# Chunked attention and a Swish feed-forward on one core: AV joined with the next scores, two halves turned by DMA, and the DMA queues planned anew

## The chip, the cores and the metric

The kernel runs on one core of a Trainium2 chip. The metric is the time on the device in microseconds (us), as the median of several executions. The kernel before took 303.95 us (302.63 to 308.57, four runs). Wherever two kernels are compared as a ratio, it is the mean time of one kernel's fast runs over the mean of the other's fast runs of the same rounds, so it is not quite the ratio of the medians that stand beside it. Differences of under 2% count as "same"; where less is claimed, the 95% interval is given.

Engines in the lines of the profile: PE is TensorE's matmul, PEld its weight load, DVE is VectorE, ACT ScalarE, POOL GpSimd, SP SyncE (here it only issues DMAs). A "q" after the name is the engine's sequencer.

## The reference, cut to what matters

```python
# q, k, v: (8 batches, 8 heads, 576 tokens, 64), float32; attention inside chunks of 64 tokens
scores = q_c @ k_c.T / 8 ; attn = softmax(scores) ; x = attn @ v_c      # x: 4608 tokens x 512
h = x @ w_in                                                            # 512 -> 2048
out = (h * sigmoid(beta * h)) @ w_out                                   # 2048 -> 512
```

The two dense products are nearly all the work. The kernel cuts the 4608 tokens into 9 blocks of 512, and each block into two halves of 256 tokens (halves 0 to 17). A block's first product (called mm1) needs both of its halves through attention; its second product (mm2) is interleaved with mm1 of the next block.

## The kernel before

The instructions' order on each engine is not written by hand. While the kernel is built, every piece of work is put into a list with its dependencies and an estimated time, and a small simulation on the host (called "the planner" here) plays the list through. The order in which its simulated engines start the pieces becomes the fixed order of the real ones. The chip then follows this order whatever happens: each engine waits for the semaphores of its next instruction and does nothing else meanwhile.

```python
def schedule(self):                       # the planner, at build time
    ...
    if kind == "dma":                     # us = (issue time on the queue, packets, ns of one packet)
        free[e] = t + us[0]
        u["packets"], u["ns"], u["arrive"] = us[1], us[2], t + 2.0
    ...
    # one DMA server for both queues, at most 64 packets at a time:
    server = t + m * u["ns"] * 1.07e-3
    ... finished(u, server + 0.9)
    # engines: among what is ready at the time, PE, SP and POOL take the lowest rank
    u = min(ready, key=lambda u: (u["rank"] ..., u["seq"]))
# [...]
P.dma(queue, (0.62, 64, 21.5), ...)       # v: half of a half's v
P.dma("sp", (2.5, 128, 27), ...)          # q and k of a half turned by a DMA transpose
P.dma("sp", (1.23, 64, 21), ...)          # x of a half turned by a DMA transpose
```

A half goes this way. SP loads q, k, v (256 KB DMAs). POOL casts q and k to bf16. Halves 0 to 5 are transposed on PE, halves 6 to 17 by a DMA transpose on SP's queue, after which POOL reorders them (two copies into `qkO`). Then PE computes the scores, ACT the exponentials, PE the product with v (AV), DVE divides by the row sum, and x is turned once more (PE or DMA) into `xT`, which mm1 reads.

```python
def attention(h, turn, ...):              # h < 6: turn == "pe", else "dma"
    ...                                   # casts, transposes, reorders
    go(r, scores, h, (0, 1), slack=0.5)   # 32 matmuls of 64x64 on four quadrants of the array
    go(0, exp, h, (0, 1))
    go(r, attend, h, (0, 1), slack=0.4)   # AV: 32 matmuls of 64x64
    for u in range(2):
        go(0, normalize, h, u)
    go(-2, turn_x_dma, h)
```

PSUM's eight banks: A0, A1 for scores, A2, A3 (and A0, A1 again) for AV, F0, F1 for mm1, F2, F3 for mm2.

The softmax here doesn't subtract the row's maximum and nothing guards it: scores larger than these inputs give would overflow.

## Time and profile before

| | before |
|---|---|
| median, us | 303.95 |
| span of the profiled run, us | 300.3 |
| PE busy | 93% |
| granted TensorE clock | 1.00 |

These are lines of the page of the kernel before: the span, the busy times (us, share of the span, instructions), then the span in 40 equal slices with PE's busy share and the granted TensorE clock in tenths, and the share of each engine in the chain of work that ended last.

```profile
span 300.3 us, 6155 instructions
...
PE 279.9 (93%) x2544; PEld 143.9 (48%) x2578; DVE 144.8 (48%) x264; ACT 153.6 (51%) x242; POOL 113.6 (38%) x117
...
PE   0799997999999999999999999999999999999995
...
PEclk9999999999999999999999999999999999999999
...
PE 86%; DMA 5%; DVE 4%; issue 2%; POOLq 1%; ACT 1%; SPq 0%; POOL 0%; DVEq 0%
```

PE is busy from the second slice to the last. The longest waits of PE in the kernel before (who waited for whom, us in total, times, longest):

```profile
PE F L482 <- DVE qkb L332: 7.7, 1, 7.7
PE A L527 <- ACT E L536: 1.4, 2, 0.7
...
PE A L527 <- POOL qkO L332: 0.8, 1, 0.8
```

The first wait is the start of the kernel. After it PE hardly ever waits for attention's data; its one wait for POOL's reorder is 0.8 us. This is how one half stands in PE's stream (start, duration, engine, line, what, how many): L605 is mm1, L634 mm2, L527 scores, L552 AV.

```profile
128.64 0.81 PE L605 MATMUL F<-xT,w_in_bf 128*128 128x512 bf16 x3
129.38 0.44 PE L527 MATMUL A<-qkO 64*64 64x64 bf16 x32
129.76 1.04 PE L605 MATMUL F<-xT,w_in_bf 128*128 128x512 bf16 x4
...
132.46 0.45 PE L552 MATMUL A<-v_bf,E 64*64 64x65 bf16 x32
```

A dense matmul of 512 columns starts every 0.216 us, and attention's two visits of about 0.5 us each lie between them without an idle gap.

### The profile page before, as it was taken

To read this page: it belongs to the slowest core of one execution; us is meant where nothing else is said; L and a number is where in the kernel's file an instruction comes from. 1 tells how busy PE (TensorE), PEld (TensorE's weight loads), DVE (VectorE), ACT (ScalarE), POOL (GpSimd) and SP (SyncE) were. 2 spreads that over 40 slices of the span, in tenths; PEclk is the share of its full clock that TensorE was granted. 3 is DMA by queue.
4 is the path that set the end of the run, shared out by engine and by line. 5 is a ranking of instruction groups with operands and counts; after the bars stand their busy time and mean duration, and the time that the engine had idled before them with its cause. 6 is when DMAs were issued, how large, how long until landed. Compare 5 with 4: busy or idle time off the path is not lost.

```text
span 300.3 us, 6155 instructions
## 1 busy us (share of the span) xinstructions
PE 279.9 (93%) x2544; PEld 143.9 (48%) x2578; DVE 144.8 (48%) x264; ACT 153.6 (51%) x242; POOL 113.6 (38%) x117
## 2 busy tenths in 40 slices
PE   0799997999999999999999999999999999999995
PEld 0575444666654444444444444444444444444444
DVE  0467905685547633464555645355353453443300
ACT  2548614875656724564664555554455545545311
POOL 1534344436576570665636375512512410000000
PEclk9999999999999999999999999999999999999999
DMA  6999399899998998999999999457636622111133
GB/s 225 283 386 403 113 294 289 255 274 263 264 264 221 214 218 186 248 191 219 222 198 251 177 256 181 103 129 160 155 108 148 132 52 55 37 35 35 46 87 79
DMA packets 94795, 55.98 MB, mean 186 GB/s; under 512 B 77736, under 2 KB 78000, under 8 KB 94768
## 3 DMA queue, kind: packets, MB, share of 16 engines
q1 hardware_dynamic: 94016, 54.41, 74.9%
q10 hardware_dynamic: 752, 1.19, 1.3%
q8 instruction: 20, 0.33, 0.4%
q14 instruction: 7, 0.06, 0.1%
HBM read 36.71 MB, written 9.44 MB: 154 GB/s over the span
## 4 chain that ended last, share of the span: by engine, by line
PE 86%; DMA 5%; DVE 4%; issue 2%; POOLq 1%; ACT 1%; SPq 0%; POOL 0%; DVEq 0%
PE F L634 38%; PE F L605 30%; PE F L609 5%; PE A L605 3%; PE A L527 3%; PE A L552 2%; DMA qkstage<-in_q_dram 2%; DMA qkT<-qkb 2%; DVE qkO L332 1%; DVE xn L566 1%; PE A L482 1%; PE A L574 1%; DMA wstage<-in_v_dram 1%; PE F L482 1%; POOLq L830 1%
## 5 line engine op out<-in xcount | busy, mean ns | idle before, releaser
L634 PE MATMUL F<-w_out_bf,g 128*128 128x512 bf16 (+1 forms) x558 | 136.0, 373 | 2.6 <-issue 1.1
L625 DVE SCALAR_TENSOR_TENSOR g<-tt,F 128x512 bf16<-128x512 bf16 (+1 forms) x148 | 91.7, 628 | 96.4 <-ACT tt L622 96.2
L622 ACT ACTIVATE tt<-F,beta_half 128x512 bf16<-128x512 f32 (+1 forms) x148 | 93.6, 641 | 86.9 <-PE F L605 78.7
L605 PE MATMUL F<-xT,w_in_bf 128*128 128x512 bf16 x448 | 111.2, 379 | 0.0
L634 PEld LDWEIGHTS F<-w_out_bf,g 128*128 128x128 bf16 x592 | 56.5, 98 | 61.2 <-DVE w_out_bf L332 0.2
L605 PEld LDWEIGHTS F<-xT,w_in_bf 128*128 128x128 bf16 x448 | 42.1, 98 | 50.8 <-DVE g L625 5.6
L332 POOL COPY qkO<-qkT 128x1024 bf16<-128x1024 bf16 x24 | 46.5, 1967 | 29.5 <-DMA qkT<-qkb 29.5
L332 POOL CAST qkb<-qkstage 128x1024 bf16<-128x1024 f32 x30 | 30.7, 1041 | 37.3 <-DMA qkstage<-in_q_dram 26.9
L330 ACT ACTIVATE ostage<-F 128x512 f32<-128x512 f32 (+1 forms) x36 | 21.3, 591 | 24.3 <-PE F L634 24.3
L332 POOL CAST v_bf<-vstage 128x512 bf16<-128x512 f32 x32 | 19.5, 613 | 20.1 <-DMA vstage<-in_v_dram 19.9
L566 DVE TENSOR_TENSOR xn<-A,R 128x512 bf16<-128x512 f32 x36 | 24.9, 691 | 1.2
L536 ACT ACTIVATE E<-A 128x512 bf16<-128x512 f32 (+1 forms) x24 | 19.4, 808 | 8.8 <-PE A L527 8.8
L609 PE MATMUL F<-xT,w_in_bf 128*128 128x256 bf16 x160 | 20.5, 273 | 0.0
L609 PEld LDWEIGHTS F<-xT,w_in_bf 128*128 128x128 bf16 x160 | 14.9, 98 | 3.5 <-DVE g L625 0.9
L564 DVE RECIPROCAL R<-A 128x8 f32<-128x8 f32 x36 | 7.3, 202 | 16.8 <-PE A L552 16.3
L527 PE MATMUL A<-qkO 64*64 64x64 bf16 x576 | 9.4, 199 | 4.4 <-ACT E L536 1.4
L332 POOL CAST qkb<-wstage 128x1024 bf16<-128x1024 f32 x4 | 4.2, 1040 | 22.6 <-DMA wstage<-in_k_dram 13.6
L527 PEld LDWEIGHTS A<-qkO 64*64 64x64 bf16 x576 | 6.7, 110 | 12.4 <-issue 4.7
L482 PE MATMUL F<-ident,qkb 128*128 128x128 bf16 x32 | 3.8, 312 | 7.7 <-DVE qkb L332 7.7
L605 PE MATMUL A<-xT,w_in_bf 128*128 128x512 bf16 x48 | 10.7, 379 | 0.0
L332 DVE COPY qkO<-A 128x1024 bf16<-128x1024 bf16 x4 | 4.9, 1224 | 10.5 <-PE A L482 10.5
L552 PEld LDWEIGHTS A<-v_bf,E 64*64 64x64 bf16 x576 | 6.6, 109 | 6.6 <-ACT tt L622 3.0
(43 smaller groups left out, 98.5 us busy)
## 6 DMA issues: line engine op xcount, KB each, us to landing
out_dram<-ostage SPq DMA_DIRECT2D x70, 128.0 KB, 2.4
qkstage<-in_q_dram SPq DMA_DIRECT2D x32, 256.0 KB, 4.4
vstage<-in_v_dram SPq DMA_DIRECT2D x32, 256.0 KB, 5.1
qkstage<-in_k_dram SPq DMA_DIRECT2D x28, 256.0 KB, 4.5
wstage<-in_moe_w_in_dram SPq DMA_DIRECT2D x4, 1024.0 KB, 13.2
g<-in_moe_w_out_dram SPq DMA_DIRECT2D x2, 1024.0 KB, 12.4
qkstage<-in_k_dram ACTq DMA_DIRECT2D x4, 256.0 KB
vstage<-in_moe_w_out_dram SPq DMA_DIRECT2D x1, 1024.0 KB, 15.0
```

Source lines behind the costliest of these rows:

```text
L330: P.op("act", us, lambda e: e.activation(dst, src, AF.Copy, **kw), reads, writes)
L332: P.op(eng, us, lambda e: e.tensor_copy(dst, src), reads, writes)
L482: P.op("pe", 0.056, lambda e, i=i: e.transpose(dst[:, i, :], qkb[:, s, which, i, :], ident[:, :]), reads=[K("qkb", s, which, i // 4, v=h), ...
L527: return e.matmul(bank(hb)[64 * c2:64 * c2 + 64, 64 * i:64 * i + 64], qkO[r, s, 1, hp, 64 * c:64 * c + 64], qkO[r, s, 0, hp, 64 * c:64 * c ...
L536: P.op("act", act_us(128 * (b - a)), lambda e: e.activation(E[:, s, :, a:b, :].rearrange("p g i q -> p g (i q)"), A[:, 0:2, 64 * a:64 * b] ...
L552: return e.matmul(bank((A2, A0)[u] + c2)[64 * hb:64 * hb + 64, j:j + 65], E[r, s, hb, i, :], v_bf[r, sv, 2 * hv + cp, 4 * hb + hp, 0:65])
L566: P.op("dve", 0.7, lambda e: e.tensor_tensor(xn[:, s, u, :, :, :].rearrange("p c k (h d) -> p c (k h) d", h=2), o[:, :, :, 0:64], R[:, 2 * ...
L605: return e.matmul(bank(n).rearrange("p (v c t) -> p v c t", v=2, c=4), w, xT[:, sx, :, u, :, 64 * hb:64 * hb + 64], start=(kt == 0), stop= ...
L609: return e.matmul(bank(n)[:, 256 * hv:256 * hv + 256].rearrange("p (c t) -> p c t", c=4), w, xT[:, sx, hv, u, :, 64 * hb:64 * hb + 64], st ...
L622: P.op("act", 0.075 + act_us(N), lambda e: e.activation(tt[:, T % 3, c], bank(n)[:, c], AF.Tanh, scale=beta_half[:, t:t + 1]), reads=[K("p ...
L625: P.op("dve", dve_us(N), lambda e: e.scalar_tensor_tensor(g2[:, sg, t, c], tt[:, T % 3, c], 1.0, bank(n)[:, c], ALU.add, ALU.mult), reads= ...
L634: P.op("pe", 0.2158 * (b - a) / 512, lambda e, t=t: e.matmul(bank(n)[:, 0:b - a], g2[:, sg, t, 128 * s:128 * s + 128], w_out_bf[:, t, a:b] ...
```

## The change

Its intent was to save PE time and to start loads better:

1. AV of half h (from 8 on) is joined with the scores of half h + 1 to one visit, so that PE changes its tiling half as often. The last two of the sixteen pairs of results find no room in A2 and A3 and take bank F3; mm2 keeps F2 alone from block 2 on. Both row halves of the array write that bank, so the second of them is put after the scores with a wait on PE's own semaphore.
2. Halves 4 and 5 are turned by DMA and POOL instead of by PE.
3. The start: v of half 0 is loaded before q and k of half 1, over two queues, and halves 0 and 1 are cast and turned in another order. A layout in which v holds token pairs is in the code but switched off ("v kept in one-token rows").
4. Loads of halves 6 to 15 wait for a gate (the Swish step) of an earlier block instead of standing in line.
5. The planner's estimates of DMA time are replaced.

The diff also holds three smaller things: the planner's cost of PE's visits is raised (by 0.2 us for a scores visit of a steady half, 0.4 for its AV, 0.2 for a joined visit), DMA transposes go first among SP's ready pieces instead of standing in line with the loads (`go(-3, turn_dma, h)` in the cut), and mm1 waits for both parts of a half's x.

```diff
-                u["packets"], u["ns"], u["arrive"] = us[1], us[2], t + 2.0
+                u["packets"], u["ns"] = us[1], us[2]
+                u["arrive"] = t + (2.0 if t < 5 else max(1.2, us[0] - 1.0))
 # estimates (issue us, packets, ns of a packet):
-  load_v     (0.62, 64, 21.5)      +  load_v     (0.62, 64, 15.3)
-  load_w_in  (0.62, 32, 91)        +  load_w_in  (0.62, 32, 86)
-  load_w_out (0.62, 16, 176)       +  load_w_out (0.62, 16, 149)
-  turn_dma   (2.5, 128, 27)        +  turn_dma   (2.5, 128, 14.6)
-  turn_x_dma (1.23, 64, 21)        +  turn_x_dma (1.23, 64, 16)
-  put        (0.6, 4, 92)          +  put        (0.6, 4, 78)
 # [... PSUM banks renamed, layouts of xn and xT, pair path (off) ...]
+        def attend_and_score(h):
+            first = attend_main(h)            # 30 of 32 AV matmuls
+            scores(h + 1, (0, 1), A0, 0)
+            attend_rest(h, first)             # the last 2, after `first` has ended
+        FIRST = 8 ; TURNED = 4 ; PAIRS = False
+        def steady(h):
+            ...
+            go(-3, turn_dma, h)               # before: in line with the loads
+            if h < FIRST + 1:
+                go(r, scores, h, (0, 1), slack=0.4)
+            else:
+                go(r, attend_and_score, h - 1, slack=0.4)
+                go(0, normalize_all, h - 1)
+                go(-2, turn_x_dma, h - 1)
 # [...]
-                        load_half(h)
+                        load_half(h, after=gated[divmod(16 * (blk - 1) + (TA, TB)[h % 2], 16)])
-                m = F3 if blk == 2 else F2 + s % 2
+                m = (F3 if blk == 2 else FS[2 + s % 2]) if 2 * blk + 2 < FIRST else F2
```

## The prediction

> **What bounds the kernel.** TensorE (PE): the page gives it 93% of a 300.3 us span, no other engine over 51%; the chain of waits is 86% PE. In the chain a run of four 128x512 matmuls takes 0.86 us, 0.216 each; the two dense products need 1152, 249 us. The other 51 us, from the start times in the engine timeline: 20.5 us before the first dense matmul (L609), 3.5 us after the last start, the rest attention between dense matmuls, with its stalls.
>
> A steady half holds PE twice (scores x32, AV x32) for 0.5 us. Only 0.27 us of that is matmuls (8.3 ns each); 0.09 us is lost before, 0.035 inside, 0.12 after. The Trainium skill, "TensorEngine Tiling (Array Packing)", Key Properties, says that a change of tiling mode drains TensorE; the trace agrees: 0.25 us per visit. Halves 4 (60.7 to 68 us) and 5 (78 to 87 us), turned on PE, each add 24 transposes (1.3 us) and about 1.7 us of lost starts, waiting in the timeline for DVE qkO (0.45) and DVE xn (0.5): 3.5 us against 1.0 for a steady half.
>
> **What changes.**
> 1. Joining AV of halves 8 to 16 with scores of 9 to 17: nine visits fewer, 9 x 0.245 = -2.2 us. The unit that waits for PE's own semaphore comes some 60 matmuls later: no bubble.
> 2. Halves 4, 5 by DMA: 2 x (3.5 - 1.0) = -5 us of PE work. But block 2 waits for a longer chain: half 5's loads land at 69.4 us; two Pool casts (1.04), DMA transpose (5.5), two Pool reorders (1.97), scores, exp, AV, division and x's transpose (4.1) end near 89 us; block 2's dense work began at 87.6 before. PE, with 7 us of block 1's mm2 as filler, would get there near 88: a stall of 0 to 3 us, +1.5.
> 3. Start: v of half 0 before q, k of half 1, over two queues: dense work 0.5 to 1.5 us earlier, and the weights with it: -1.
> 4. The join takes a PSUM bank: mm2 of blocks 2 to 7 has F2 alone, so each of 24 swaps waits for ACT's eviction (0.59 us, behind a tanh of 0.64), which one mm1 group (0.86 us) mostly hides: 0.05 us each, +1.2.
> 5. Queues: DMA is near 1.0 busy from 40 to 190 us, but steady blocks are barely starved (one loss of 0.99 us at 239.5): 0.
>
> "One-token rows" changes nothing: the pair path is switched off.
>
> **Sum.** -5.5 us: 298.4 us, 80% range 295 to 302. Faster by over 2% 0.36, within 2% 0.61, slower 0.03.
>
> **What would show it.** (1) Joined visits of 0.8 us instead of 2 x 0.5, nine fewer. (2) 32 q/k and 16 x transposes fewer on PE; whether block 2's first mm1 waits for a DMA of xT. (3) The first 128x256 matmul near 19.5 us. (4) PE waiting for ACT ostage at the first matmul of an mm2 group. (5) PE waiting for Pool qkO near 240 us: the last halves had 5 us of slack, which a faster PE eats.
>
> **What would make it wrong.** If halves 4, 5 are loaded earlier, step 2 brings all 5 us (below 297). If transposes slow the loads in the busiest DMA stage, block 2 stalls by over 3 us. If a swap stalls 0.2 us, the gain of joining is gone.

## The result, and the profile after

The changed kernel took 329.88 us (329.18 to 332.46, four runs), ratio 1.0884 with a 95% interval of 1.0803 to 1.0966: 26 us slower, far outside the predicted range of 295 to 302. The same lines of its page:

```profile
span 327.6 us, 6075 instructions
...
PE 287.6 (88%) x2499; PEld 145.1 (44%) x2530; DVE 144.0 (44%) x264; ACT 151.3 (46%) x234; POOL 119.6 (37%) x119
...
PE   1579989989759989996999799868999999999996
...
PEclk9999999999976999998799999996999999999999
...
PE 48%; DMA 24%; POOL 11%; SPq 7%; issue 4%; DVE 2%; ACT 2%; ACTq 1%; POOLq 0%
```

PE's row has holes all along, and the chain that ended last, 86% PE before, is now only 48% PE: it runs through DMA, POOL and the queue. The granted clock is cut in three places of the row. PE's waits after:

```profile
PE A L587 <- POOL qkO L334: 15.8, 8, 4.2
PE F L492 <- DVE qkb L334: 8.4, 3, 6.7
PE F L702 <- DMA xT<-xn: 3.9, 1, 3.9
```

L587 is the scores, L702 mm1. Eight times PE arrives at a half's scores and POOL has not yet written that half's `qkO`. One such visit in the engine timeline of the changed kernel (L610 is AV, L731 mm2), and the entry to block 2:

```profile
90.38 0.59 PE L587 MATMUL A<-qkO 64*64 64x64 bf16 x32 [2.29 <-POOL qkO L334]
90.91 2.65 PE L731 MATMUL A<-w_out_bf,g 128*128 128x512 bf16 x6
...
94.35 0.47 PE L610 MATMUL A<-v_bf,E 64*64 64x65 bf16 x32
98.68 5.28 PE L702 MATMUL F<-xT,w_in_bf 128*128 128x512 bf16 x12 [3.86 <-DMA xT<-xn]
...
149.99 0.44 PE L610 MATMUL A<-v_bf,E 64*64 64x65 bf16 x30
153.68 0.64 PE L587 MATMUL A<-qkO 64*64 64x64 bf16 x32 [3.25 <-POOL qkO L334]
154.13 0.24 PE L610 MATMUL A<-v_bf,E 64*64 64x65 bf16 x2
154.30 1.89 PE L702 MATMUL F<-xT,w_in_bf 128*128 128x512 bf16 x4
```

The bracket holds the idle time before an instruction and what ended it. At 150 us the 30 AV matmuls run, PE stands for 3.25 us, and only then come the scores and the last two AV matmuls. After it four mm1 matmuls take 1.89 us instead of 1.03: the clock is halved. The Trainium skill, "TensorE: Matmul & The Clock Gate", "What's actually happening", says that an idle window of some 3.4 us takes the array to half rate until it has been busy for as long. The trace agrees on the half rate and on how it ends: after this stall dense matmuls start 0.427 us apart instead of 0.216 until 159.3 us, for about 5 us. It does not need a whole idle window, though: the clock was cut at 152.47 us, when PE had been idle for 2.0 us (more on this in the last section).

Summed over the start times in the trace (after the start-up, gaps over 0.55 us before a PE instruction beyond its normal spacing): 22.9 us of stalls and 7.6 us at half clock in the changed kernel, against 5.2 and 0 in the kernel before. That is 25.3 of the 27.3 us between the two spans. So the loss is PE waiting for attention's data, and the clock that follows from it. The question is why the data come late.

Since the order comes from the planner, its simulated times can be set beside the trace. This table holds, for odd halves, the end of POOL's second reorder, after which the scores can start (us; read from the planner as the kernel is built, and from the trace; the two last kernels are experiments below):

```
half                              7      9     11     13     15
before            planned     101.7  126.5  150.5  176.1  192.0
                  on the chip  98.0  124.1  149.6  176.0  192.1
changed           planned      89.8  111.9  133.5  160.5  192.2
                  on the chip 100.0  126.7  153.6  184.7  222.5
before_fast       planned      86.1  104.1  121.4  137.9  151.9
                  on the chip  94.6  117.8  139.9  162.1  180.8
const             planned     106.5  128.6  150.1  180.5  210.4
                  on the chip 103.6  123.5  146.8  180.3  212.4
```

In the kernel before the chip is up to 4 us ahead of the plan, so PE finds its data ready. In the changed one it is 10 us behind at half 7 and 30 us behind at half 15. The planner had promised 295.9 us for the changed kernel and 295.2 us for the one before.

### The profile page after: what moved, and what is told of

It reads as the page before. It is cut to its first block, busy times and chain, and to the rows that moved or that the text cites. A ratio compares the mean times of both kernels' runs of the same rounds, so it can differ in the third digit from the quotient of the medians.

```text
span 327.6 us, 6075 instructions
## 1 busy us (share of the span) xinstructions
PE 287.6 (88%) x2499; PEld 145.1 (44%) x2530; DVE 144.0 (44%) x264; ACT 151.3 (46%) x234; POOL 119.6 (37%) x119
## 3 DMA queue, kind: packets, MB, share of 16 engines
q1 hardware_dynamic: 98208, 55.46, 69.4%
## 4 chain that ended last, share of the span: by engine, by line
PE 48%; DMA 24%; POOL 11%; SPq 7%; issue 4%; DVE 2%; ACT 2%; ACTq 1%; POOLq 0%
PE F L731 21%; PE F L702 17%; DMA qkT<-qkb 12%; DMA vstage<-in_v_dram 9%; POOL qkO L334 9%; PE A L731 4%; SPq L403 3%; DMA qkstage<-in_q_dram 3%; PE F L706 2%; ACT tt L719 2%; PE A L587 2%; DVE g L722 1%; POOL qkb L334 1%; ACTq L403 1%; SPq L426 1%
## 5 line engine op out<-in xcount | busy, mean ns | idle before, releaser
L731 PE MATMUL F<-w_out_bf,g 128*128 128x512 bf16 (+1 forms) x474 | 118.0, 379 | 2.0 <-issue 0.9
L702 PE MATMUL F<-xT,w_in_bf 128*128 128x512 bf16 x448 | 115.9, 394 | 3.9 <-DMA xT<-xn 3.9
L731 PEld LDWEIGHTS F<-w_out_bf,g 128*128 128x128 bf16 x496 | 48.0, 99 | 56.0 <-issue 2.3
L702 PEld LDWEIGHTS F<-xT,w_in_bf 128*128 128x128 bf16 x448 | 43.6, 101 | 59.4 <-issue 10.2
L334 POOL CAST qkb<-qkstage 128x1024 bf16<-128x1024 f32 (+1 forms) x30 | 30.4, 1027 | 45.9 <-DMA qkstage<-in_q_dram 40.2
L599 ACT ACTIVATE E<-A 128x1024 bf16<-128x1024 f32 (+1 forms) x19 | 17.7, 933 | 24.6 <-PE A L610 15.5
L649 DVE TENSOR_TENSOR xn<-A,R 128x512 bf16<-128x512 f32 (+2 forms) x36 | 24.9, 691 | 1.2
L332 ACT ACTIVATE ostage<-F 128x512 f32<-128x512 f32 x30 | 17.9, 597 | 14.0 <-PE F L731 13.8
L587 PE MATMUL A<-qkO 64*64 64x64 bf16 x544 | 9.0, 206 | 17.5 <-POOL qkO L334 15.8
L731 PE MATMUL A<-w_out_bf,g 128*128 128x512 bf16 (+1 forms) x87 | 21.3, 379 | 1.0 <-issue 0.7
L587 PEld LDWEIGHTS A<-qkO 64*64 64x64 bf16 x544 | 6.9, 117 | 22.4 <-POOL qkO L334 14.8
L731 PEld LDWEIGHTS A<-w_out_bf,g 128*128 128x128 bf16 x96 | 9.3, 101 | 8.4 <-issue 1.6
L719 ACT ACTIVATE tt<-A,beta_half 128x512 bf16<-128x512 f32 (+1 forms) x17 | 10.5, 640 | 3.5 <-PE A L702 1.9
L722 DVE SCALAR_TENSOR_TENSOR g<-tt,A 128x512 bf16<-128x512 bf16 (+1 forms) x17 | 10.3, 620 | 1.6 <-ACT tt L719 1.3
L610 PEld LDWEIGHTS A<-v_bf,E 64*64 64x64 bf16 x576 | 7.5, 113 | 7.6 <-issue 6.3
```

Of the source, the lines that this page charges most:

```text
L332: P.op("act", us, lambda e: e.activation(dst, src, AF.Copy, **kw), reads, writes)
L334: P.op(eng, us, lambda e: e.tensor_copy(dst, src), reads, writes)
L587: return e.matmul(bank(b + hb)[64 * c2:64 * c2 + 64, 64 * i:64 * i + 64], qkO[r, s, 1, hp, 64 * c:64 * c + 64], qkO[r, s, 0, hp, 64 * c:64 ...
L599: P.op("act", act_us(128 * (b - a)), lambda e: e.activation(E[:, s, :, a:b, :].rearrange("p g i q -> p g (i q)"), S[:, :, 64 * a:64 * b], ...
L610: return e.matmul(bank(n)[64 * hb:64 * hb + 64, 65 * j:65 * j + 65], E[r, s, hb, i, :], v_bf[r, sv, 2 * hv + cp, 4 * hb + hp, 0:65])
L649: P.op("dve", 0.15 + 1.05e-3 * n, lambda e: e.tensor_tensor(dst, o[..., 0:64], r.unsqueeze(len(r.shape)).to_broadcast(shape), ALU.mult), r ...
```

## The experiments

Theories. A: the new estimates of DMA time make a plan that the chip can't keep, and engines that work in a fixed order wait. Rivals. B: the join, since AV now waits for the next half's scores and mm2 has one bank less. C: halves 4 and 5 by DMA. D: loads tied to gates, which hand lateness on from half to half. All kernels gave correct results.

### First round: one part undone at a time

**const**: the changed kernel with the old estimates and the old arrival rule, nothing else.

```diff
-  the new estimates (seven numbers) and the arrival rule shown in "The change"
+  those of the kernel before
```

> The changed kernel with only the planner's estimates of DMA time set back to those of before (v packet 15.3 to 21.5 ns, q/k transpose 14.6 to 27, x transpose 16 to 21, and the others; arrival again issue + 2.0 us). Nothing on the chip is moved but the static order. Theory A (the order is planned with DMA times that the chip does not keep, so PE meets its attention visits before Pool qkO is there, and an in-order engine waits): the waits of PE for Pool qkO, 15.8 us after, fall below 5, the clock stays at 1.0, and the time falls to about 312 or less; the planner itself then says 310 against 296. Theories B (the join), C (halves 4 and 5 by DMA), D (loads tied to gates): the same mechanisms are all there, so it stays within 5 us of 330.

Measured: 313.47 us, ratio to before 1.0349 [1.0305, 1.0393]. 16 us come back by changing numbers that no instruction contains. The lateness of half 15 falls from 30 to 2 us (table above), the clock stays up but for one place, and the waits of PE become:

```profile
PE F L492 <- DVE qkb L334: 9.7, 2, 6.7
PE F L702 <- DMA xT<-xn: 5.4, 2, 4.9
PE F L731 <- ACT ostage L332: 2.1, 3, 0.7
...
PE A L587 <- POOL qkO L334: 0.4, 1, 0.4
```

The wait for POOL's `qkO` has gone from 15.8 to 0.4 us. What is left are waits of other kinds: block 2's first mm1 for `xT`, and mm2 (L731) for ACT to empty its only bank. The planner itself says 310.0 us for this kernel, against 295.2 for the kernel before, so a loss of this size was in the plan already.

**nojoin**: the changed kernel without the join; mm2 has two banks again.

```diff
-        FIRST = 8
+        FIRST = 18
-            else:
+            elif FIRST <= 2 * LAST + 1:
                 go(450, attend_all, 2 * LAST + 1, slack=0.4)
```

> The changed kernel with the join switched off: AV and scores of every half are visits of their own again, and mm2 has its two banks. Theory B (AV waits for the next half's scores and one bank less for mm2): the joined stalls of 0.7 to 4.4 us (12 us, and 5 us of halved clock behind them) go, time about 313. Theory A: the scores still come before their qkO, so the stalls stay, now before the scores visit: 325 to 330.

Measured: 327.04 us, 1.0774 [1.073, 1.0819]. The stalls stay, now before scores visits of their own:

```profile
PE A L587 <- POOL qkO L334: 15.3, 7, 4.0
```

The profiled run is slow (330.65 us, where the fastest took 325.41), so only its kind of wait is used here, not its length. B is not the main cause.

**pe45**: halves 4 and 5 turned on PE again.

```diff
-        TURNED = 4
+        TURNED = 6
```

> The changed kernel with halves 4 and 5 turned on PE again. Theory C (the loss is from the longer DMA chain of halves 4, 5 in the busiest DMA stage): the stalls of 2.5 and 4.0 us at 88 to 99 us and the 6 us of halved clock behind them go, 5 us of PE work comes back, and all later stages come earlier: about 318. If the loop of theory A or D goes on by itself, the later joined stalls (12 + 5 us) stay: also about 320 to 324; under C alone they go as well, near 308.

Measured: 322.71 us, 1.0652 [1.059, 1.0714]. The entry to block 2 is mended (no stall there over 0.7 us), and 7 us come back, but PE still waits for POOL `qkO` later on:

```profile
PE A L587 <- POOL qkO L334: 13.6, 8, 3.6
```

C is a part, not the cause.

**ungate**: the loads of halves 6 to 15 stand in line again.

```diff
-                        load_half(h, after=gated[divmod(16 * (blk - 1) + (TA, TB)[h % 2], 16)])
+                        load_half(h)
```

> The changed kernel with the loads of halves 6 to 15 in line again instead of behind a gate of the block before. Theory D (a load that waits for a gate comes as late as PE is, so lateness is handed on from half to half and never made up): the lateness of Pool's qkO against the plan, which grows from 5 us at half 4 to 31 us at half 17, stays below 15, and the time falls to about 312. Theory A: the order still meets late data; some gain, but not under 320.

Measured: 330.6 us, 1.0902 [1.0852, 1.0952]. No gain, and half 15 is 29.6 us late as before. D falls, as far as the growing lateness goes.

### Second round: the estimates alone, and what they leave

**before_fast**: the converse of const. The kernel before, with nothing but the new estimates and the new arrival rule.

```diff
-  P.dma(queue, (0.62, 64, 21.5), ...)  -  P.dma("sp", (2.5, 128, 27), ...)    # and the others
+  P.dma(queue, (0.62, 64, 15.3), ...)  +  P.dma("sp", (2.5, 128, 14.6), ...)
```

> The kernel before, with nothing but the planner's DMA estimates and arrival rule of the changed kernel put in. The planner then promises 291.8 us instead of 295.2. Theory A (the loss is made by an order planned with DMA times the chip does not keep): slower than before by 10 us or more, 313 to 325, with PE waiting for Pool qkO by over 8 us in all and Pool's qkO ever later against the plan. If the estimates do harm only together with the change's other parts: within 3 us of 303.

Measured: 326.21 us, 1.0786 [1.0703, 1.0868], just above the 313 to 325 that theory A gave. The estimates alone make the kernel before 23.6 us slower. Its waits of PE (L528 is the scores):

```profile
PE A L528 <- POOL qkO L333: 17.7, 8, 3.4
PE F L483 <- DVE qkb L333: 6.6, 1, 6.6
```

In before_fast half 11 is ready at 139.9 us, ten microseconds *earlier* than in the kernel before (149.6), and still the kernel is 23.6 us slower. The attention data are not slow; PE's order asks for them too soon. The 384th dense matmul (256-column ones counted as half, scaled for records that are missing in the trace) starts at 121.5 us in the kernel before and at 135.2 in before_fast, although both had started the 224th at 82.5 us (82.6 and 82.4). With a fixed order, a visit that the plan puts too early holds up the dense work behind it, which could have filled the time; from then on PE goes at the pace of the DMA chain, and dense work is left over for the end.

**const_pe45**, **const_nojoin** and **const_pe45_nojoin**: the changed kernel with the old estimates and one or both of the other parts undone.

```diff
+  the old estimates, as in const
-        TURNED = 4      # const_pe45, const_pe45_nojoin
+        TURNED = 6
-        FIRST = 8       # const_nojoin, const_pe45_nojoin
+        FIRST = 18      # and the guard of nojoin
```

> The changed kernel with the old estimates and with halves 4 and 5 turned on PE; join, gated loads and start as changed. Theory A plus C: what is left of the loss under the old estimates (10 us) is mostly the entry to block 2, so the stall of 5.1 us before block 2's first mm1 and the halved clock behind it go: 304 to 307. If the join or the start is the rest instead: 310 or more.

Measured: 311.35 us, 1.0292 [1.0214, 1.0369].

> The changed kernel with the old estimates and without the join (mm2 has two banks again). What the join is worth when the order is sound: if it brings the 2.2 us of nine saved visits net, this is about 315.5; if the single mm2 bank (PE and its weight loads wait 4 us for ACT ostage with the join) takes it back, 311 to 313.5.

Measured: 312.79 us, 1.0332 [1.0256, 1.0408].

> The changed kernel with the old estimates, halves 4, 5 on PE and no join: only the start, the gated loads and the priorities of the queues are left of the change. If these are neutral, as predicted: 303 to 305. If the start or the gating costs by itself: 306 or more.

Measured: 309.08 us, 1.0176 [1.0089, 1.0263]; the verdict is "unclear", since the interval crosses 2%.

Each by itself brings little (2.1 and 0.7 us against const, with intervals that overlap const's), both together 4.4 us, and 6 us stay. const_pe45 was expected at 304 to 307 if the entry to block 2 was most of what is left; it is not. const_nojoin came out as expected if the single bank takes back what the join brings. The last was expected at 303 to 305 if the rest is neutral, and is above that. Every edit gives the planner another order, so parts do not add up neatly.

### Third round: one part alone on the kernel before

These three start from the kernel before, its old estimates included, so each shows what a part is worth in an order that holds.

**join_only**: the join and the one bank for mm2.

```diff
-                go(r, scores, h, (0, 1), slack=0.5) ... go(r, attend, h, (0, 1), slack=0.4)
+                attend_and_score(h - 1) from half 9 on; m = F2 from block 3 on
```

> The kernel before with the join alone (AV of halves 8 to 16 with the scores of the next, mm2 of blocks 2 to 7 in one PSUM bank); old start, old loads, old estimates. If the prediction's step 1 and step 4 are right (nine visits of 0.245 us fewer, 24 bank swaps of 0.05 us): 301.5 to 303. If a swap costs as much as the 0.85 us stalls seen under the old estimates, it is 305 or more. The planner says 302.2 against 295.2.

Measured: 307.5 us, 1.0121 [1.0043, 1.0198]: slower by 3.9 us, not faster. (Compared at equal granted clock it is slower too: by 3.3 us among runs at 0.999 or 1.0, by 4.5 us among runs at 0.994.) The join itself does what was predicted, though it brings less. This is a joined visit in the engine timeline of join_only, then one of its bank swaps:

```profile
130.32 0.44 PE L610 MATMUL A<-v_bf,E 64*64 64x65 bf16 x30
130.58 0.49 PE L587 MATMUL A<-qkO 64*64 64x64 bf16 x32
130.89 0.22 PE L610 MATMUL A<-v_bf,E 64*64 64x65 bf16 x2
131.04 1.90 PE L702 MATMUL F<-xT,w_in_bf 128*128 128x512 bf16 x8
```

```profile
111.89 1.24 PE L731 MATMUL F<-w_out_bf,g 128*128 128x512 bf16 x5
113.82 3.63 PE L731 MATMUL F<-w_out_bf,g 128*128 128x512 bf16 x16 [0.69 <-ACT ostage L332]
```

From the first AV to the next mm1 the visit takes 0.72 us, with no bubble before the last two matmuls. Counted from the dense matmul before it to the one after, less the normal spacing, a visit takes 0.47 us of PE in the kernel before, and a joined one 0.81 us instead of twice that: 0.13 us saved for each, 1.2 us for nine, where 2.2 us were predicted. The way in and out is saved nearly as predicted (0.21 us for each visit less), but inside, the matmuls of a joined visit start 9.3 ns apart instead of 8.2. (In some visits the record of the first dense matmul after them is missing, as its weight load shows; these are left out.)

Against that, mm2 stops for 0.69 us at 113.1 us while ACT empties F2 (a 0.60 us copy). Between 112 and 232 us the spacing lost between one dense matmul and the next, about 0 in the kernel before, is some 5 us in join_only. Half of it is such bank swaps: four of the 24 stop PE, 2.6 us in all. Most of the rest, 2.0 us in four waits, is PE waiting for DVE's `g`, the Swish step. Before the one that ends at 171.4 us the gate stood on DVE behind the joined division, whose multiplication takes 1.09 us at once where the kernel before has two of 0.69 us.

**start_only**: the new start.

```diff
-        for parts in ("q", "v"): ...load q, k of both halves, then v on one queue
+        for h in range(2): load_half(h, "sp", "act")
+        turn(0, FS); score(0); turn(1, FS); average(0, (F2, F3)); score(1, F0); average(1)
```

> The kernel before with the new start alone (v of half 0 before q, k of half 1, v over two queues, the new order of turning, scores and AV of halves 0 and 1). Step 3 of the prediction: 301 to 302.5. If the rest of const_pe45_nojoin's loss of 6.5 us (3.7 to 5 us behind at the 64th to 96th dense matmul) comes from the start: 305 to 309.

Measured: 303.85 us, 1.0023 [0.9949, 1.0097], between the two ranges expected. No difference can be told. The 96th dense matmul starts 4 us later than before (45.4 against 41.4 us), but by the 128th it is 1.2 us later, since the kernel before loses the difference between them anyway, where its 128th waits for half 2 and for the last piece of w_out.

**dma45_only**: halves 4 and 5 by DMA.

```diff
         for h in (4, 5):
-            attention(h, "pe", (A0, A1), None, ("act", "dve"))
+            attention(h, "dma", None, None, None)
```

> The kernel before with halves 4 and 5 turned by DMA alone. Step 2 of the prediction: -3.5 us, 299. If the chain of half 5 into block 2 costs what it costs under the old estimates in the changed kernel (5.1 us of stall and the halved clock behind it, against 5 us of PE work saved): 304 to 309. The planner says 306.2.

Measured: 312.92 us, 1.0317 [1.0247, 1.0386]: slower by 9.4 us, more than the 304 to 309 expected. The engine timeline of dma45_only at the entry to block 2:

```profile
90.66 0.45 PE L610 MATMUL A<-v_bf,E 64*64 64x65 bf16 x32 [1.23 <-ACT E L599]
98.66 4.12 PE L702 MATMUL F<-xT,w_in_bf 128*128 128x512 bf16 x12 [7.55 <-DMA xT<-xn]
```

PE has saved the transposes (its 224th dense matmul starts 3.3 us earlier than before, 79.3 against 82.6), runs out of work and stands 7.55 us until half 5's x lands; the first ten dense matmuls after that run at half clock, 2.1 us more. With the 1.23 us shown above and two waits for ACT `ostage` (1.2 us) that makes 8.8 of the 9.4 us.

**const_turns**: the changed kernel with only the estimates of the two DMA transposes set back.

```diff
-  turn_dma (2.5, 128, 14.6)    turn_x_dma (1.23, 64, 16)
+  turn_dma (2.5, 128, 27)      turn_x_dma (1.23, 64, 21)
```

> The changed kernel with only the two estimates of DMA transposes set back (14.6 to 27 and 16 to 21 ns a packet). Theory A holds with any of the estimates; this asks which does it. If the transposes carry it: 313 to 317, as with all set back (313.5). If the loads and the arrival rule count as much: 320 to 325.

Measured: 320.29 us, 1.0547 [1.0485, 1.0609]; half 15 is 18.8 us late. The transposes' estimates carry 9.6 of the 16.4 us that all of them do; the loads' and the arrival rule carry the rest.

### Fourth round: rate or landing

The new estimates are not careless. From issue to landing, medians over those DMAs whose landing the trace shows (the loads are those of halves 6 to 15; v loads, not shown, take 0.2 to 1.2 us longer than the new plans say):

```
                       q or k load        q/k transpose      x transpose
                      planned  chip      planned  chip      planned  chip
before                  6.00   4.44        8.12   5.52        6.50   4.10
before_fast             3.97   3.96        5.19   5.58        3.61   3.45
changed                 3.06   3.52        4.40   5.05        3.20   3.10
```

For a single DMA the new plan is the better one, and it is the old that is wrong by half. What differs is the pace. From half 6 to half 15 the plan of before expects one half per 11.3 us, the plan of before_fast one per 8.2 us; with that order the chip delivered one per 10.6 us (85.1 to 180.8 us over nine halves). Two edits of before_fast tell rate from landing.

**fast_rate132**

```diff
-                    server = t + m * u["ns"] * 1.07e-3
+                    server = t + m * u["ns"] * 1.32e-3
```

> The kernel before with the new estimates, and the planner's DMA server slowed from 1.07 to 1.32 of the packets' sum. The plan then brings Pool's qkO of halves 6 to 15 one every 10.4 us, where the chip brought one every 10.6 us under the new estimates and the unslowed plan expected one every 8.2. If the rate is what was wrong: no growing lateness, 302 to 306. If landing is: still over 315.

Measured: 312.98 us median, 1.0226 [1.0123, 1.0328] of before. The four runs were 307.93, 312.41, 313.56 and 313.74 us; on one core the two slowest and the profiled one are slow only because they are over 1.5% above the fastest, so the verdict is unclear in size. In the profiled run half 15 is 7.4 us late, and PE waits 6.4 us for `qkO`.

**fast_late2**

```diff
-                        finished(u, server + 0.9)
+                        finished(u, server + 2.9)
```

> The kernel before with the new estimates, and 2 us more between a DMA's last packet and its landing in the planner. The plan's halves still come one every 8.7 us. If the rate is what was wrong: the lateness still grows to 25 us or more and the time stays at 318 to 326. If a margin on each DMA is enough: 303 to 310.

Measured: 322.73 us, 1.0608 [1.0539, 1.0678]; half 15 is 24.3 us late, and PE waits 15.2 us for `qkO`. Two more microseconds on every DMA cure 3.5 of 23.6 us; slowing the planner's DMA rate alone cures 13 us by the medians. So the planned rate is the greater part. It was expected to be all of it, and is not: fast_rate132 planned one half per 10.4 us, and its chip delivered one per 11.5 us (91.7 to 195.2 us), so the pace that the chip keeps is not one number but depends on the order. Both edits start from the kernel before. In the changed kernel, whose loads wait for gates, the plan expects one half per 12.5 us and the chip delivers one per 14.7, so how its loss splits between rate and landing was not tested.

The traces show which queue keeps the pace. Apart from a few DMAs of the start and the end, all loads, transposes and stores pass through SP's queue in order. This is a stretch of it in the engine timeline of before_fast, with no gap over 0.1 us:

```profile
111.87 0.61 SPq L402 DMA_DIRECT2D qkstage<-in_q_dram  x1
112.53 0.60 SPq L402 DMA_DIRECT2D qkstage<-in_k_dram  x1
113.17 0.60 SPq L402 DMA_DIRECT2D qkstage<-in_q_dram  x1
113.82 0.60 SPq L402 DMA_DIRECT2D qkstage<-in_k_dram  x1
114.47 1.57 SPq L417 DMA_DIRECT2D vstage<-in_v_dram  x2
116.08 4.55 SPq L497 DMA_TRANSPOSE qkT<-qkb  x1
120.67 1.31 SPq L588 DMA_TRANSPOSE xT<-xn  x1
122.02 1.75 SPq L656 DMA_DIRECT2D out_dram<-ostage  x2
```

From the q/k transpose of half 6 to that of half 15 the DMA instructions occupy SP for 90.3 of 94.3 us on the chip, where the plan has 69.2 of 72.9 us for the same instructions. So the 21 us of lateness gained on the way are the 21 us by which they hold the queue longer than planned: 11.6 us are the nine q/k transposes (3.8 us each, planned at 2.5), 5.2 us the x transposes, 3.8 us the stores. In the kernel before they hold it for 90.4 us as well, planned at 75.3, but there the slow estimates left the queue 25 us of slack in a plan of 100.8 us, which took up the difference. In fast_rate132 it is 100.2 of 104.8 us, with one more x transpose and six more stores on the way. Neither set of estimates corrected these issue times (2.5 and 1.23 us), and no run did. The time of an x transpose or a store can include a wait for its data. For the q/k transposes that is not it: each starts after POOL's casts for it have ended (of half 8 at 88.1 us, its transpose starts at 94.4 and holds SP for 5.04 us). Why they hold the queue so long is not shown.

**before_rate10**: the kernel before with 1.00 in place of 1.07, one half per 10.5 us in the plan.

> The kernel before with the planner's DMA server at 1.00 instead of 1.07: one half every 10.5 us in the plan instead of 11.3. The chip needs about 10.6, so the order is planned just at the edge: 302 to 306, neither much better nor much worse; if the margin of before was too large, 300 to 302.

Measured: 304.05 us, 1.0024 [0.9962, 1.0086]. The order is as good as before's. It leads at first (its 160th dense matmul starts at 62.9 us, before's at 65.2) and loses the lead in one stall of 2.0 us that ends at 206.8 us, where half 16 is 7.7 us late.

**all_but_start**: const_pe45_nojoin with the loads in line instead of gated.

```diff
-                        load_half(h, after=gated[...])
+                        load_half(h)
```

> The changed kernel with the old estimates, no join, halves 4, 5 on PE, and the loads in line instead of gated. Gated it took 309.1. If the gating is what is left: 303 to 305. If it is the rest (start, transposes put first in the queue, the planner's dearer visits): 308 to 310.

Measured: 306.39 us, 1.0048 [0.9989, 1.0107], against 1.0176 [1.0089, 1.0263] gated. The intervals overlap a little, so the gating probably costs some 1%, but this is not shown beyond doubt. The kernel still contains the dearer visits, the transposes first and mm1's wait for both parts of x, so these and the new start together cost about 1% at most.

### Fifth round: the plan mended where the traces show it wrong

The table shows where the plan of the kernel before is off: up to half 11 the chip is ahead, and the last two halves come 3 and 6.6 us late. Their 40 loads are small, and most hold SP's queue for 0.63 to 0.75 us in the trace, where the plan has 0.62. **ramp_a** and **ramp_b** put that right in the kernel before.

```diff
-                    server = t + m * u["ns"] * 1.07e-3
+                    server = t + m * u["ns"] * (1.00e-3 if t < 80 else 1.07e-3)   # ramp_b: t < 100
-                P.dma(queue, (0.62, 2, 92), ...)       -  P.dma(queue, (0.62, 32, 21.5), ...)
+                P.dma(queue, (0.72, 2, 92), ...)       +  P.dma(queue, (0.68, 32, 21.5), ...)
```

> The kernel before with three of its planner's numbers put right after the traces: DMA server at 1.00 of the packets' sum up to 80 us (before_rate10 was 2.3 us ahead of before at the 160th dense matmul), 1.07 as before after that (before_rate10 lost that lead to a stall of 2.0 us at 205 us), and the issue time of the last halves' small loads 0.72 and 0.68 us instead of 0.62. If lateness at the visits is what costs: no stall over 1 us after 100 us, 300.5 to 302 against 303, that is 0.3 to 0.8% faster. If the rest of before's stalls have other causes: within 0.3%.

> The same with the switch from 1.00 to 1.07 at 100 us instead of 80: 300.5 to 302.5 by the same reasoning, with a little more risk of a late qkO between 140 and 200 us.

Measured in five rounds: ramp_a 300.34 us, 0.9946 [0.991, 0.9982]; ramp_b 300.44 us, 0.9938 [0.9894, 0.9983]; the kernel before 302.19 us in these rounds. Both are a little faster than the kernel before, by about 0.6%, under 2% but clear of zero. Part of it is the clock: four of the eleven runs of the kernel before have a granted clock of 0.994 (303.7 us in the mean), none of the twelve of ramp_a and ramp_b has. Against the other seven (301.8 us) the two gain 1.0 us. The two mended numbers were not tried apart. From the page of ramp_a:

```profile
span 298.2 us, 6192 instructions
...
PE 282.7 (95%) x2578; PEld 143.8 (48%) x2578; DVE 145.2 (49%) x264; ACT 153.1 (51%) x242; POOL 114.4 (38%) x117
```

PE's busy share is 95%. The same instructions as in the kernel before, in a slightly other order.

## Why the prediction was wrong, point by point

**Step 5, "Queues: ... 0", is the step that failed.** The prediction looked only at whether the steady blocks were starved by the DMA engines, and counted the new DMA estimates nowhere. It overlooked that the planner's numbers fix the order on all five engines. Alone on the kernel before they cost 23.6 us; set back in the changed kernel they return 16.4 us. In before_fast the chain is shown at each link: the plan's pace (8.2 us a half against 10.6 on the chip), SP's queue (occupied for 90.3 of 94.3 us, planned for 69.2), the growing lateness of `qkO` (29 us at half 15), PE's wait for it (17.7 us), the half clock after the longest stalls. That PE can't go round a waiting visit agrees with the Trainium skill, "TensorE: Matmul & The Clock Gate", "The mechanism", which calls the matmuls "strict FIFO, no reordering": in the 3.25 us before 153.68 us no matmul was run.

**Step 2 (-3.5 us predicted) had the wrong sign: +9.4 us alone.** The saving on PE was there: 3.3 us by the 224th dense matmul. The stall was put at 0 to 3 us and is 7.55 us, with 2.1 us of half clock behind it. The mis-sized term is the chain of half 5. Its casts ended at 68.8 us, before the landing of its loads that the prediction assumed (69.4), but its DMA transpose was issued only at 77.2 us, behind half 6's loads and two stores on the same in-order queue. The prediction summed the durations of the links and forgot the wait in the queue between them. x landed at 98.5 us, not "near 89".

**Steps 1 and 4 (-2.2 and +1.2 us predicted) came out at +3.9 us together.** Step 1's mechanism is right in kind: nine visits fewer, 0.72 us for a joined one, no bubble at the self-wait. Its size was about double: 0.13 us saved for each instead of 0.245. Step 4 is the term that was mis-sized most: some 5 us were lost between dense matmuls from 112 to 232 us. The 24 swaps were put at 0.05 us each; most cost nothing, but four stop PE for 0.5 to 0.7 us, 2.6 us in all, and the waits for DVE's `g` (2.0 us) are in no step.

**Step 3 (-1 us) is within the noise**: 1.0023 [0.9949, 1.0097].

**"One-token rows changes nothing"** was right as far as it goes: the pair path is off in the changed kernel, so no run tested it.

**What the prediction named as a danger** is what happened in part ("if a swap stalls 0.2 us, the gain of joining is gone"; "block 2 stalls by over 3 us"), but the range allowed for neither, let alone for both, and the largest cause was not on the list.

**What the planner would have told.** Under the old estimates its totals are 295.2 us for the kernel before, 302.2 with the join, 306.2 with halves 4 and 5 by DMA and 294.7 with the new start, that is +7.0, +11.0 and -0.5 us, where +3.9, +9.4 and +0.3 were measured. Building each part by itself would have warned of steps 1, 2 and 4 before any run. Of the new estimates it could not warn: with them it promised 291.8 us.

**Still open.** SP's queue is the place where the pace is lost, but why its q/k transposes hold it for 2 to 5 us each is not known; no experiment gave the planner the measured issue times, or measured the DMA engines by themselves. The parts do not add: alone they make 23.6 + 9.4 + 3.9 + 0.3 = 37.2 us, together 25.9. Once PE waits at one visit, the time of another cause is partly hidden in that wait; that is an argument, not a measurement. And 6 us that const_pe45_nojoin keeps are at most half explained, by the gating. The planner's dearer visits are a rival that no run set back (with the old costs of visits the plan of this kernel is 298.6 instead of 308.4 us).

## What to carry to other kernels

In a kernel whose order is fixed when it is built, an estimate of time is part of the program: check the planned time of each hand-over against the trace, half by half, before believing the planned total, and give the shared DMA queue a margin, since a visit planned too early costs PE its whole wait, while planning some a few microseconds late cost the kernel before little (0.6% came back in ramp_a). More exact estimates of single DMAs made the plan worse here, because they removed the margin that had covered another wrong number, the time for which a transpose holds the queue. So when one estimate of a queue is mended, compare the others of that queue with the trace too. And before work is moved off the busiest engine, add up the new chain with its places in the in-order queues, not only with the durations of its links.

## What the Trainium skill lacked or had wrong

- "TensorEngine Tiling (Array Packing)", "Key Properties", says that a change of tiling mode drains TensorE, with no size. Here a visit of 64x64 matmuls between dense ones lost 0.093 us on the way in and 0.117 us on the way out.
- "TensorE: Matmul & The Clock Gate", "Why this matters for your kernels", asks for no idle gaps over about 3 us. That was no boundary here: in the changed kernel a gap of 2.29 us before 90.38 us was followed by half rate from 91.03 us, while in before_fast a gap of 3.36 us before 94.77 us was not. The same page says that the window runs freely, and the traces bear that out: the clock record changes on a grid of 3.41 us. What the page does not say is how much idleness in a window is enough. The window of 87.62 to 91.03 us held 67% of idle PE; the gap of 3.36 us fell on two windows with 49% and 52%. In all kept traces together, each full-rate window with 57% of idle PE or more was followed by half rate, and none with 46% or less was; between them both happened.
- None of the pages has the pace of a mixed stream of loads, stores and DMA transposes on one queue. Here the stream delivered one half per 10.6 to 11.5 us, where a plan whose median times for q and k loads and transposes were within 0.4 us of the measured ones expected 8.2 and a plan slowed as a whole 10.4. In before_fast a q/k transpose held the issuing queue for 3.8 us in the mean, an x transpose for 2.1, a q or k load for 0.6.
- "DMA: Bandwidth & Descriptors", "Latency and other measured facts", gives DMA_TRANSPOSE 261 GB/s in one kernel. The q/k transpose of one half here moves 0.5 MB (128 partitions x 2048 bf16 elements) in a median of 5.05 to 5.58 us from issue to landing among other traffic, about 100 GB/s by division. Of this, 2.8 to 3.5 us (medians) pass while the issuing instruction still holds SP's queue, so this is no rate of the transfer alone; for the length of a chain it is the number to take.
